# Attention to mixture in one kernel: v loaded two units ahead, a 13th early weight tile, and two small loads on another queue

## The chip, the cores and the metric

One core of a Trainium2 chip runs the whole program. The metric is the device time of one execution in microseconds (us), lower is better. All arithmetic is float32 or forms of it.

## What is computed

Three steps follow one another: a linear attention with decay over 4 batches and 8 heads, a soft mixture of 8 experts over the 3072 tokens that come out of it, and a two-layer block with `h - tanh(h)` between its layers.

```python
for b in range(nb):                                   # attention, blocks of the sequence
    intra = einsum('bhij,bhjd->bhid', (qb @ kb.T) * Dmask, vb)
    inter = einsum('bhid,bhde->bhie', qb * lam_pow, kv_state)
    out[:, :, sl] = intra + inter
    kv_state = lam_block * kv_state + einsum('bhsd,bhse->bhde', kb * rev_pow, vb)

logits = x @ phi                                      # x: attention's output, (3072, 512)
slot_input = softmax(logits, 0).T @ x                 # (32, 512)
for e in range(8):
    slot_out[e] = relu(slot_input[e] @ w1[e]) @ w2[e] # w1: 512 x 1024, w2: 1024 x 512
x = softmax(logits, 1) @ slot_out

h = x @ w_in                                          # 512 x 2048
out = (h - tanh(h)) @ w_out                           # 2048 x 512
```

## The kernel before

**Stages.** The order of all instructions is written out by hand. The attention runs 24 units u (6 blocks of 128 positions, `c = u // 4`, times 4 batches). The loop at lines 437 to 490 is skewed: iteration u holds `scores(u + 1)` (q times k), `route(u - 1)` (the output turned, and once in four units the logits) and `attend(u)` (times v, and the state). After the last unit follows a short tail that forms `si`, the slots' inputs. Then come 8 experts (`expert1`, `expert2`), PE's first matmul of them being `hp`. Then the last block, whose 96 chunks (`dps`, `s`, `r`, `ops`) need `w_in` and `w_out` decoded from 64-bit words (`wif`, `wf`, line 121) first.

**Loads.** All loads are issued by SP, in the order of the code. A unit needs `qk` (512 KB), `v` (256 KB) and, up to unit 19, k in another layout: either loaded (256 KB) or, for the units in `TURN_K`, turned on PE by `turn_k` (4 transposes) and copied by ScalarE. `load_unit(u, 0)` loads qk, `load_unit(u, 1)` k and v. Iteration u issues qk(u + 3), then `FILL[u]` half tiles of expert weights (512 KB each), then k(u + 3) and v(u + 3). qk, k and v have three buffers each, so v(u + 3) goes where v(u) lay and waits for `attend(u)`.

**The ring of weight tiles.** A weight tile is 1 MB (8 KB per partition), loaded as two halves. Tiles come from groups that become free at different times: `a` (3 tiles) and `b` (12) exist from the start, `d` (1) opens after iteration 19 in the space of the k tiles, `e` (1) after iteration 22 in that of the qk tiles, `c` (4) after the last unit in that of the rest of the attention. `RING_OF` names the group of each load in turn: 21 tiles in all before the first is used again. Tile 22 (`w1_5_1`, of expert 5) goes into an `a` tile and waits for the first matmuls `hp` of expert 0.

**In flight.** A load's issue also waits for the landing of the load eight before it, whose semaphore it takes over. So up to eight are in flight, and they land in the order of their issue.

**Start.** SP issues `lam` (4 KB), then qk and v of units 0, 1 and 2, then `phi` in four pieces of 16 KB.

Of the kernel before, what the change touches and what calls it, by code (L numbers as in the profile page):

```python
# [9 lines left out]
F32 = mybir.dt.float32  # L10
# [10 lines left out]
B, H, S, DH = 4, 8, 768, 64  # L21
P = 128
NC = S // P
NP = H // 2
DM = H * DH
# [6 lines left out]
NU = NC * B  # L32
# [30 lines left out]
LATE = 8,  # L63
LINEAR = 43, 47
CHECK = 57, 59, 63
TURN_K = [0, 1, 2, 6, 11, 16]
FILL = [2, 1, 1, 1, 1, 2, 2, 1, 1, 1, 2, 1, 1, 2, 1, 2, 1, 2, 1, 2, 3, 2, 6, 8]
RING = dict(a=3, b=12, d=1, e=1, c=4)
RING_OF = "a" * 3 + "b" * 12 + "de" + "c" * 4 + "a" * 3 + "b" * 8


@with_exitstack
def tile_main(ctx, tc, qkv, lam, phi, w1, w2, w_in, w_out, out):
    nc = tc.nc
# [135 lines left out]
    with pool("att_out") as att_out:  # L210
# [4 lines left out]
        att_qk = with_q.enter_context(pool("att_qk"))  # L215
        att_k = with_state.enter_context(pool("att_k"))
# [14 lines left out]
        qk_t, kc_t, sd_t, xt_t, xn_t = {}, {}, {}, {}, {}  # L231
        lt_ps, dn_t, al_t, dt_t = {}, {}, {}, {}

        def load_unit(u, part=None):
            if part in (None, 0):
                qk_t[u] = att_qk.tile([P, 2, NP, P], F32, tag="qk", name="qk", bufs=3)
                nc.sync.dma_start(
                    out=qk_t[u].rearrange("p t a i -> p t (a i)"), in_=qkv[u, :, 0:2])
            if part in (None, 1):
                if u // B < NC - 1 and u not in TURN_K:  # L240
                    k_t[u] = att_k.tile([P, DM], F32, tag="k", name="k", bufs=3)
                    nc.sync.dma_start(out=k_t[u], in_=qkv[u, :, 2])
                v_t[u] = v_t.get(u) or new_v()
                nc.sync.dma_start(out=v_t[u], in_=qkv[u, :, 3])

        def turn_k(u, qk, bk):
            if u in TURN_K:
# [44 lines left out]
        def attend(u):  # L292
            c, b = divmod(u, B)
            v, at = v_t.pop(u), at_t.pop(u)

            xp = [bank(3 + h2, [P, 2, P], "xp") for h2 in range(2)]
            at_head = lambda p, h2: xp[h2][p % 2 * DH:(p % 2 + 1) * DH, p // 2]
            if c > 0:
                for p in range(NP):
                    for h2 in range(2):  # L300
                        sl = slice(h2 * DH, (h2 + 1) * DH)
                        nc.tensor.matmul(  # L302
                            at_head(p, h2), st_t[b][sl, p], qs_t[u][sl, p], start=p < 2, stop=False,
                            skip_group_check=True)
            xt_t[u] = att_out.tile([P, 2, 2, P], F32, tag="xt", name="xt", bufs=5)
            for h2 in range(2):
                for p in range(NP):
                    h = 2 * p + h2
                    nc.tensor.matmul(  # L309
                        at_head(p, h2), v[:, h * DH:(h + 1) * DH], at[:, h],  # L310
                        start=c == 0 and p < 2, stop=True, skip_group_check=True)
                nc.scalar.copy(xt_t[u][:, h2], xp[h2])  # L312
            if c < NC - 1:
                up = bank(7, [P, NP, DH], "up")
                for p in range(NP):
                    for h2 in range(2):
                        h = 2 * p + h2
                        nc.tensor.matmul(  # L318
                            up[h2 * DH:(h2 + 1) * DH, p], kc_t[u][:, h],
                            v[:, h * DH:(h + 1) * DH], start=True, stop=True)  # L320
                if c == 0:
                    nc.vector.tensor_copy(st_t[b], up)
                else:
                    nc.vector.tensor_tensor(out=st_t[b], in0=up, in1=sd_t[u], op=ALU.add)  # L324
# [70 lines left out]
                    out=acc, in0=acc, scalar=al_t[c], in1=ap, op0=ALU.mult, op1=ALU.add)  # L395


        nc.sync.dma_start(out=lamb[:, :H], in_=bass.AP(tensor=lam.tensor, offset=lam.offset, ap=[[0, P], [1, H]]))
        load_unit(0, 0)
        load_unit(0, 1)  # L400
        load_unit(1, 0)
        load_unit(1, 1)
        load_unit(2, 0)
        load_unit(2, 1)
        for h2 in range(2):
            for g in range(2):
                nc.sync.dma_start(
                    out=phi_sb[g * DH:(g + 1) * DH, 2 * h2:2 * h2 + 2],
                    in_=phi[h2 * DH:(h2 + 1) * DH].rearrange("d (s g) n -> d s g n", g=2)[:, :, g])

# [25 lines left out]
                channel_multiplier=1)  # L436
        for u in range(-1, NU):
            if 3 <= u + 3 < NU:
                load_unit(u + 3, 0)
            if u >= 0:  # L440
                fill(FILL[u])
            if 3 <= u + 3 < NU:
                load_unit(u + 3, 1)
            if u + 1 < NU:
                scores(u + 1)
            if u < 0:
                turn_k(0, qk_t[0], 4)
                turn_k(1, qk_t[1], 5)
                prep_q(0)
                prep_q(1)  # L450
                prep_k(0)
            if 2 <= u + 2 < NU:
                prep_q(u + 2)
            late_route = (u - 1) // B == NC - 1
            if u >= 1 and not late_route:
                route(u - 1)
            last_of = u - 1 if u >= 1 and (u - 1) % B == B - 1 else None
            if last_of is not None:
                mm = route_max(last_of // B)
            if u >= 5 and u % B == 1:  # L460
                route_t((u - 5) // B)
            if 0 <= u < NU:
                attend(u)
                if u == 0:
                    for h2 in range(2):
                        sl = slice(h2 * DH, (h2 + 1) * DH)
                        nc.vector.tensor_copy(
                            lamb[sl, H:], lamb[sl, :H].rearrange("p (a j) -> p a j", j=2)[:, :, h2])
                    for p in range(NP):
                        powers(ql[:, p], lamb[:, H + p:H + p + 1], nil, 1.0)  # L470
                if u + 2 < NU:
                    turn_k(u + 2, qk_t[u + 2], 6 if u else 5)
                if u + 1 < NU:
                    prep_k(u + 1)
            if late_route:
                route(u - 1)
            if last_of is not None:
                route_exp(last_of // B, *mm)
            if u >= 5 and u % B == 1:
                route_acc((u - 5) // B)  # L480
            if u == NU - B - 1:
                with_state.close()
                open_ring("d", only_early, reuse_waits="tile")
            if u == NU - 2:
                with_q.close()
                open_ring("e", only_early, reuse_waits="tile")
            if u == NU - 1:
                in_attention.close()
                open_ring("c", only_early, reuse_waits="tile")
                fill()  # L490
# [37 lines left out]
        for k in range(KD):  # L528
            nc.tensor.matmul(
                sip[:, k], acc[:, k * P:(k + 1) * P], gf[:, 1], start=k == 0, stop=False,  # L530
                skip_group_check=True)
        aps = att_out.tile([P, DM], F32, tag="xt", name="aps", bufs=5)
        nc.vector.tensor_copy(aps[:, :256], ap[:, :256])
        nc.scalar.copy(aps[:, 256:], ap[:, 256:])
        for k in range(KD):
# [612 lines left out]
```

## Time and profile before

| | us |
|---|---|
| median of three runs (313.27 to 317.07) | 314.67 |
| the profiled execution, its own time | 315.38 |
| its span, first to last instruction | 313.6 |
| attention, to the last matmul with v | 109.7 |
| first matmul of the experts | 117.8 |
| first matmul of the last block | 159.1 |

The profiled execution is 1.8 us longer than its span, and 0.7 us above the median. Shares of the span: PE (TensorE) 94% busy, DVE (VectorE) 58%, ACT (ScalarE) 43%, POOL (GpSimd) 36%. TensorE's granted clock is full nearly throughout (0.996 on the mean), which is the 2.4 GHz level. A row of the timeline gives start, length, engine, line, operation, and what is written from what; in brackets stands the idle time ahead of it and who ended it.

### The profile page before, as it was taken

What the parts mean: (1) busy time and instruction counts of PE and PEld (TensorE: products, weight loads), DVE (VectorE), ACT (ScalarE), POOL (GpSimd) and SP (SyncE); (2) the same over time, 40 slices, a digit from 0 to 9 for tenths busy, and PEclk for the clock granted to TensorE, in tenths of its full rate; (3) what the DMA queues carried; (4) which work ended last, traced back from release to release, by engine and by line L of the source; (5) the groups of instructions that cost most, each with busy time, mean ns of one, the idle gap of its engine ahead of it and who ended that gap; (6) DMA issues with size and microseconds to landing.
All of it is one profiled execution on the core that took longest, in us unless ns stands there. A gap on an engine that the chain in (4) does not pass through costs nothing.

```text
span 313.6 us, 7419 instructions
## 1 busy us (share of the span) xinstructions
PE 294.5 (94%) x2999; PEld 212.6 (68%) x2999; DVE 181.2 (58%) x329; ACT 133.9 (43%) x280; POOL 112.9 (36%) x163
## 2 busy tenths in 40 slices
PE   7979999999999999999989889999999899999991
PEld 7868777877877774444356567777754677787771
DVE  4844435544553334520069759597773877968782
ACT  1434333334423332232239578576632544444420
POOL 3347647674673104110276545677500001000000
PEclk9999999999999999999999999999999999999998
DMA  6999999999999989999989847463000030303254
GB/s 202 369 399 381 370 403 368 382 382 380 387 380 386 382 267 408 397 392 401 394 319 336 299 146 287 161 244 134 2 2 0 2 134 0 134 2 134 76 192 141
DMA packets 33256, 79.77 MB, mean 254 GB/s; under 512 B 3649, under 2 KB 3905, under 8 KB 33217
## 3 DMA queue, kind: packets, MB, share of 16 engines
q1 hardware_dynamic: 33216, 79.25, 68.4%
q8 instruction: 25, 0.41, 0.5%
q14 instruction: 15, 0.11, 0.1%
HBM read 72.95 MB, written 6.29 MB: 253 GB/s over the span
## 4 chain that ended last, share of the span: by engine, by line
PE 44%; DMA 36%; DVE 9%; issue 4%; SPq 3%; POOL 1%; ACT 1%; DVEq 0%; POOLq 0%; ACTq 0%
PE ops L820 21%; DMA w<-in_w 19%; DMA qk<-in_qkv 12%; PE dps L795 5%; DVE r L813 4%; DMA wi<-in_w_in 3%; PE xp L309 3%; PE sc L285 3%; DVE part L828 2%; PE xp L302 2%; PE xnp L343 1%; PE ops L1056 1%; PE qp L872 1%; POOL top L117 1%; DMA wo<-in_w_out 1%
## 5 line engine op out<-in xcount | busy, mean ns | idle before, releaser
L820 PE MATMUL ops<-wr,r 128*128 128x512 f32 (+1 forms) x388 | 109.1, 397 | 1.2 <-ACT part L826 0.9
L820 PEld LDWEIGHTS ops<-wr,r 128*128 128x128 f32 x388 | 72.3, 188 | 22.3 <-ACT part L826 3.1
L799 ACT ACTIVATE s<-dps 128x512 f32<-128x512 f32 x96 | 56.9, 603 | 53.8 <-PE dps L795 51.3
L813 DVE SCALAR_TENSOR_TENSOR r<-dps,mt,s 128x512 fp32r<-128x512 f32 x89 | 64.9, 746 | 20.0 <-ACT s L799 19.2
L795 PE MATMUL dps<-c,ms 128*128 128x512 f32 x96 | 39.5, 425 | 3.8 <-DVE r L813 1.9
L289 DVE TENSOR_TENSOR at<-sc,dtab 128x512 f32<-128x512 f32 x48 | 30.9, 684 | 15.6 <-PE sc L285 15.6
L257 POOL TENSOR_TENSOR qs<-qk,ql 128x512 f32<-128x512 f32 x20 | 25.8, 1291 | 34.9 <-DMA qk<-in_qkv 31.7
L345 ACT COPY xn<-xnp 128x512 f32<-128x512 f32 x24 | 14.1, 586 | 43.6 <-PE xnp L343 43.6
L285 PE MATMUL sc<-qk 64*128 64x128 f32 x384 | 27.9, 285 | 4.2 <-DMA qk<-in_qkv 4.2
L285 PEld LDWEIGHTS sc<-qk 64*128 64x128 f32 x384 | 23.3, 187 | 10.7 <-DMA qk<-in_qkv 6.0
L795 PEld LDWEIGHTS dps<-c,ms 128*128 128x128 f32 x96 | 17.9, 188 | 15.2 <-DVE r L813 7.4
L309 PE MATMUL xp<-at,v 128*64 128x128 f32 x384 | 26.3, 279 | 0.0
L264 POOL TENSOR_TENSOR kc<-k,dtab 128x512 f32<-128x512 f32 x20 | 21.2, 1061 | 11.3 <-ACT k L252 5.2
L312 ACT COPY xt<-xp 128x256 f32<-128x256 f32 x48 | 17.8, 373 | 16.5 <-PE xp L309 16.0
L309 PEld LDWEIGHTS xp<-at,v 128*64 128x64 f32 x384 | 20.5, 136 | 4.1 <-issue 3.8
L324 DVE TENSOR_TENSOR st<-up,sd 128x256 f32<-128x256 f32 x16 | 6.8, 425 | 25.6 <-PE up L318 25.6
L828 DVE TENSOR_TENSOR part<-ops,part 128x512 f32<-128x512 f32 (+1 forms) x29 | 17.9, 666 | 0.9 <-PE ops L1056 0.9
L576 PE MATMUL hp<-w,si 128*32 128x256 f32 x256 | 16.1, 383 | 1.3 <-DMA w<-in_w 1.3
L117 POOL CAST top<-wi 128x512 f16<-128x512 bf16 x16 | 14.6, 922 | 6.0 <-DMA wi<-in_w_in 4.7
L600 PE MATMUL op<-w,hz 128*32 128x512 f32 x128 | 16.5, 594 | 0.0
L121 DVE SCALAR_TENSOR_TENSOR wif<-wi,top 128x512 uint32<-128x512 uint32 x16 | 13.2, 834 | 5.4 <-POOL top L117 5.4
L117 POOL CAST top<-wo 128x512 f16<-128x512 bf16 x16 | 15.1, 967 | 3.1 <-DMA wo<-in_w_out 3.1
(181 smaller groups left out, 339.9 us busy)
## 6 DMA issues: line engine op xcount, KB each, us to landing
w<-in_w SPq DMA_DIRECT2D x64, 512.0 KB, 9.2
qk<-in_qkv SPq DMA_DIRECT2D x24, 512.0 KB, 7.6
wi<-in_w_in SPq DMA_DIRECT2D x16, 512.0 KB, 4.7
wo<-in_w_out SPq DMA_DIRECT2D x16, 512.0 KB, 4.3
v<-in_qkv SPq DMA_DIRECT2D x24, 256.0 KB, 7.1
out<-part SPq DMA_DIRECT2D x23, 256.0 KB, 2.2
k<-in_qkv SPq DMA_DIRECT2D x14, 256.0 KB, 8.4
out<-part SPq DMA_DIRECT2D x2, 128.0 KB, 3.5
```

The costliest lines, as they stand in the source:

```text
L117: nc.gpsimd.tensor_copy(out=every(top().bitcast(F16), 2, 1)[:, sl], in_=every(raw().bitcast(BF16)[:, 4:], 4, 0)[:, sl])
L257: nc.gpsimd.tensor_tensor(out=qs_t[u], in0=qk_t[u][:, 0], in1=ql, op=ALU.mult)
L264: nc.gpsimd.tensor_tensor(out=kc_t[u], in0=k_t.pop(u).rearrange("p (h d) -> p h d", h=H), in1=kd, op=ALU.mult)
L285: nc.tensor.matmul(sc[h2][:, p], qk[sl, 1, p], qk[sl, 0, p], start=True, stop=True)
L289: nc.vector.tensor_tensor(out=by_head(at_t[u], h2), in0=sc[h2], in1=by_head(dtab, h2), op=ALU.mult)
L309: nc.tensor.matmul(at_head(p, h2), v[:, h * DH:(h + 1) * DH], at[:, h], start=c == 0 and p < 2, stop=True, skip_group_check=True)
L312: nc.scalar.copy(xt_t[u][:, h2], xp[h2])
L795: nc.tensor.matmul(d_t[n], ms[:, f * P:(f + 1) * P], c4[:, c], start=True, stop=True)
L799: nc.scalar.activation(out=s, in_=d_t[n], func=AF.Square, scale=math.sqrt(1.0 / 3))
L813: nc.vector.scalar_tensor_tensor(out=r_t[n], in0=d, scalar=mt[:, f, NS:], in1=s, op0=ALU.add, op1=ALU.mult)
L820: nc.tensor.matmul(op, r_t[n][:, t * P:(t + 1) * P], wr_t[f // 2][:, f % 2, sl], start=first, stop=last)
L828: nc.vector.tensor_tensor(out=pt, in0=op, in1=pt, op=ALU.add)
```

## The change

Four edits, made together.

1. `lam` and the four pieces of `phi` are issued by ScalarE's queue, ahead of anything else there.
2. `load_unit` becomes `load_qk` (qk and k) and `load_v`. Iteration u issues qk(u + 3) and k(u + 3), then the weights, then v(u + 2). Only v(0) and v(1) are loaded ahead of the loop.
3. `b` has 13 tiles and `c` 3; `RING_OF` follows, still with 21 tiles. `FILL` issues its 12th half tile one iteration later and the following ones earlier: by iteration 20 it has issued 32 halves, where it had 31. The output tiles `xt` have 4 buffers for 5, which gives 2 KB per partition back.
4. k is turned for units 0, 1, 2, 6, 10, 14 and 18 (7), not 0, 1, 2, 6, 11 and 16 (6): 13 loads of k for 14.

```diff
-TURN_K = [0, 1, 2, 6, 11, 16]
-FILL = [2, 1, 1, 1, 1, 2, 2, 1, 1, 1, 2, 1, 1, 2, 1, 2, 1, 2, 1, 2, 3, 2, 6, 8]
-RING = dict(a=3, b=12, d=1, e=1, c=4)
-RING_OF = "a" * 3 + "b" * 12 + "de" + "c" * 4 + "a" * 3 + "b" * 8
+TURN_K = [0, 1, 2, 6, 10, 14, 18]
+FILL = [2, 1, 1, 1, 1, 2, 1, 2, 1, 2, 1, 2, 1, 2, 1, 2, 1, 2, 1, 2, 3, 2, 6, 8]
+RING = dict(a=3, b=13, d=1, e=1, c=3)
+RING_OF = "a" * 3 + "b" * 13 + "de" + "c" * 3 + "a" * 3 + "b" * 8
...
-        nc.sync.dma_start(out=lamb[:, :H], ...)
-        load_unit(0, 0)
-        load_unit(0, 1)
-        load_unit(1, 0)
-        load_unit(1, 1)
-        load_unit(2, 0)
-        load_unit(2, 1)
+        nc.scalar.dma_start(out=lamb[:, :H], ...)
+        load_qk(0)
+        load_v(0)
+        load_qk(1)
+        load_v(1)
+        load_qk(2)
...
-                nc.sync.dma_start(out=phi_sb[...], ...)
+                nc.scalar.dma_start(out=phi_sb[...], ...)
...
             if 3 <= u + 3 < NU:
-                load_unit(u + 3, 0)
+                load_qk(u + 3)
             if u >= 0:
                 fill(FILL[u])
-            if 3 <= u + 3 < NU:
-                load_unit(u + 3, 1)
+            if 2 <= u + 2 < NU and u >= 0:
+                load_v(u + 2)
```

On SP, at the start of the program, the order changes as follows (a row is an instruction with its line, what it writes and from where; `-` before, `+` after; the numbers behind the names tell buffers apart).

```order
-L398 DMA lamb_96<-in_lam 128x8
-L237 DMA qk_98<-in_qkv 128x1024
+L236 DMA qk_98<-in_qkv 128x1024
 L244 DMA v_92<-in_qkv 128x512
-L237 DMA qk_101<-in_qkv 128x1024
+L236 DMA qk_101<-in_qkv 128x1024
 L244 DMA v_103<-in_qkv 128x512
-L237 DMA qk_105<-in_qkv 128x1024
-L244 DMA v_107<-in_qkv 128x512
-L407 DMA phi_sb_95<-in_phi 64x2x32 x4
-L237 DMA qk_183<-in_qkv 128x1024
+L236 DMA qk_105<-in_qkv 128x1024
+L236 DMA qk_181<-in_qkv 128x1024
```

The first load of SP is now qk(0), and qk(3) (`qk_183`, now `qk_181`) stands right behind qk(2), with v(2) and `phi` gone from between them. v(1) there and the three loads behind it now take over the semaphores of `lam` and of `phi`, and wait for their landing.

On SP, at the end of the attention, before: from qk(22) (`qk_1545`) on, with v(22) (`v_1550`), qk(23) (`qk_1609`) and v(23) (`v_1616`), the last load that the attention needs. `w1_4_0` is the tile of group `e`, `w1_4_1` the first of group `c`.

```order
L237 DMA qk_1545<-in_qkv 128x1024
L156 DMA w1_3_1_1547<-in_w1 128x1024 x2
L244 DMA v_1550<-in_qkv 128x512
L237 DMA qk_1609<-in_qkv 128x1024
L165 DMA w2_3_0_1611<-in_w2 128x2x512 x2
L165 DMA w2_3_1_1614<-in_w2 128x2x512
L244 DMA v_1616<-in_qkv 128x512
L165 DMA w2_3_1_1614<-in_w2 128x2x512
L156 DMA w1_4_0_1789<-in_w1 128x1024 x2
L156 DMA w1_4_1_1824<-in_w1 128x1024 x2
```

The same place of the changed kernel, from v(21) (`v_1555`) on: qk(23) is `qk_1614`, v(22) `v_1620`, v(23) `v_1697`. `w1_4_0` is now the tile of group `d`, `w1_4_1` that of `e`, `w2_4_0` the first of `c`.

```order
L244 DMA v_1555<-in_qkv 128x512
L236 DMA qk_1614<-in_qkv 128x1024
L165 DMA w2_3_0_1553<-in_w2 128x2x512
L165 DMA w2_3_1_1617<-in_w2 128x2x512 x2
L244 DMA v_1620<-in_qkv 128x512
L156 DMA w1_4_0_1694<-in_w1 128x1024 x2
L244 DMA v_1697<-in_qkv 128x512
L156 DMA w1_4_1_1797<-in_w1 128x1024 x2
L165 DMA w2_4_0_1832<-in_w2 128x2x512 x2
```

v(22) has moved from ahead of qk(23) to behind it and behind three halves of weights; ahead of v(23) stand 34 halves of weights, not 31, and behind it, ahead of group `c`, two halves and not three.

## Rows read from the trace of the kernel before

**Rows 1.** Chain that ended last, in time: start, length, what.

```profile
114.01 12.22 DMA w<-in_w
...
147.24 10.65 DMA wi<-in_w_in
```

**Rows 2.** Stretches: us, busy us (count) by engine, clock, DMA share, GB/s.

```profile
24.00:104.00 80.00, 78.07 (x1395) 62.86 (x1395) 37.91 (x74) 29.45 (x81) 48.09 (x51) 1.00 1.03 382
108.00:116.00 8.00, 7.79 (x104) 5.77 (x103) 2.48 (x11) 4.00 (x12) 0.00 (x0) 1.00 0.81 261
126.00:157.00 31.00, 29.69 (x330) 12.43 (x322) 6.04 (x18) 7.78 (x15) 4.25 (x10) 1.00 1.04 396
```

**Rows 3.** Timeline of SP's issues: start, length, line, what, count.

```profile
0.75 0.39 SPq L398 DMA_DIRECT2D lamb<-in_lam  x1
1.20 0.42 SPq L237 DMA_DIRECT2D qk<-in_qkv  x1
...
4.37 2.88 SPq L407 DMA_DIRECT2D phi_sb<-in_phi  x4
...
100.13 0.34 SPq L244 DMA_DIRECT2D v<-in_qkv  x1
```

**Rows 4.** Single DMA issues (from 1.20, 95.15, 100.13, 102.51, 109.80, 111.11): KB, us to landing.

```profile
qk<-in_qkv SPq DMA_DIRECT2D x1, 512.0 KB, 4.8
...
v<-in_qkv SPq DMA_DIRECT2D x1, 256.0 KB, 7.3
...
v<-in_qkv SPq DMA_DIRECT2D x1, 256.0 KB, 8.3
...
w<-in_w SPq DMA_DIRECT2D x1, 512.0 KB, 9.8
...
w<-in_w SPq DMA_DIRECT2D x1, 512.0 KB, 3.7
...
w<-in_w SPq DMA_DIRECT2D x1, 512.0 KB, 7.0
```

**Rows 5.** Waits of SP: who, for whom, us in total, times, longest.

```profile
SPq L244 <- PE up L318: 25.6, 16, 2.5
```

**Rows 6.** Timeline of PE, end of the attention and first expert.

```profile
106.42 1.09 PE L309 MATMUL xp<-at,v 128*64 128x128 f32 x16
107.44 0.66 PE L343 MATMUL xnp<-cst,xt 128*128 128x128 f32 x4
108.03 0.67 PE L302 MATMUL xp<-qs,st 64*64 64x128 f32 x16
108.62 1.09 PE L309 MATMUL xp<-at,v 128*64 128x128 f32 x16
109.65 0.66 PE L343 MATMUL xnp<-cst,xt 128*128 128x128 f32 x4
...
117.81 1.93 PE L576 MATMUL hp<-w,si 128*32 128x256 f32 x32
```

**Rows 7.** Timeline of PE, experts 6 and 7, and start of the last block.

```profile
142.22 1.93 PE L576 MATMUL hp<-w,si 128*32 128x256 f32 x32
143.97 1.90 PE L600 MATMUL op<-w,hz 128*32 128x512 f32 x16
...
146.60 1.30 PE L576 MATMUL hp<-w,si 128*32 128x256 f32 x16
...
149.83 0.64 PE L576 MATMUL hp<-w,si 128*32 128x256 f32 x8 [0.65 <-DMA w<-in_w]
150.29 1.90 PE L600 MATMUL op<-w,hz 128*32 128x512 f32 x16
...
159.11 1.10 PE L743 MATMUL mp__2401<-wif,so 128*32 128x128 f32 x16
```

**Rows 8.** Timeline of DVE, the last decode ahead of the last block.

```profile
158.83 0.69 DVE L121 SCALAR_TENSOR_TENSOR wif<-wi,top 128x512 uint32<-128x512 uint32 x1 [0.65 <-POOL top L117]
```

**Rows 9.** The page's costliest groups: busy us, mean ns of one, idle before.

```profile
L285 PE MATMUL sc<-qk 64*128 64x128 f32 x384 | 27.9, 285 | 4.2 <-DMA qk<-in_qkv 4.2
```

**Rows 10.** ACT's timeline at the start, and one turned k of PE's.

```profile
0.75 1.28 ACT L252 ACT_TABLE_LOAD   x1 [0.75 <-PEq L1138]
7.86 0.59 ACT L252 COPY k<-kp 128x512 f32<-128x512 f32 x1 [5.83 <-PE kp L250]
...
11.21 0.66 PE L250 MATMUL kp<-cst,qk 128*128 128x128 f32 x4
```

**Rows 11.** Uses of v: min/median/max ns, first and last start in us.

```profile
L309 PE MATMUL xp<-at,v x384: 272/273/323, 9.7 to 109.4; 128*64 128x128 f32 x192
```

More of the change, by code (lines that the diff above doesn't have):

```diff
@@ L232, in tile_main, with load_qk, load_v @@
         lt_ps, dn_t, al_t, dt_t = {}, {}, {}, {}
[L234 to L244, printed above, removed]
+        def load_qk(u):
+            qk_t[u] = att_qk.tile([P, 2, NP, P], F32, tag="qk", name="qk", bufs=3)
+            nc.sync.dma_start(
+                out=qk_t[u].rearrange("p t a i -> p t (a i)"), in_=qkv[u, :, 0:2])
+            if u // B < NC - 1 and u not in TURN_K:
+                k_t[u] = att_k.tile([P, DM], F32, tag="k", name="k", bufs=3)
+                nc.sync.dma_start(out=k_t[u], in_=qkv[u, :, 2])
+        def load_v(u):
+            v_t[u] = v_t.get(u) or new_v()
+            nc.sync.dma_start(out=v_t[u], in_=qkv[u, :, 3])
         def turn_k(u, qk, bk):
@@ L304, in attend @@
                             skip_group_check=True)
-            xt_t[u] = att_out.tile([P, 2, 2, P], F32, tag="xt", name="xt", bufs=5)
+            xt_t[u] = att_out.tile([P, 2, 2, P], F32, tag="xt", name="xt", bufs=4)
             for h2 in range(2):
@@ L395, in route_acc @@
                     out=acc, in0=acc, scalar=al_t[c], in1=ap, op0=ALU.mult, op1=ALU.add)
-        nc.sync.dma_start(out=lamb[:, :H], in_=bass.AP(tensor=lam.tensor, offset=lam.offset, ap=[[0, P], [1, H]]))
-        load_unit(0, 0)
-        load_unit(0, 1)
-        load_unit(1, 0)
-        load_unit(1, 1)
-        load_unit(2, 0)
-        load_unit(2, 1)
+        nc.scalar.dma_start(
+            out=lamb[:, :H], in_=bass.AP(tensor=lam.tensor, offset=lam.offset, ap=[[0, P], [1, H]]))
+        load_qk(0)
[3 more added lines that the diff above has]
+        load_qk(2)
         for h2 in range(2):
             for g in range(2):
-                nc.sync.dma_start(
+                nc.scalar.dma_start(
                     out=phi_sb[g * DH:(g + 1) * DH, 2 * h2:2 * h2 + 2],
@@ L531, in tile_main @@
                 skip_group_check=True)
-        aps = att_out.tile([P, DM], F32, tag="xt", name="aps", bufs=5)
+        aps = att_out.tile([P, DM], F32, tag="xt", name="aps", bufs=4)
         nc.vector.tensor_copy(aps[:, :256], ap[:, :256])
```

## The prediction

> **What bounds the kernel now.** I read the chain of waits first, then the stretches, then the single loads with their landing, then PE's timeline at the two ends of the experts. The chain leads through the experts by loads, `w` after `w` and then `wi` [rows 1], so up to about 158 us the end hangs on the stream of loads. The stretches say how full that stream is: 382 GB/s over the attention and 396 over the experts, with a DMA share of 1.03 and 1.04, and between them a dip to 261 GB/s [rows 2]. A rate of 382 GB/s is 0.686 us for 256 KB; I call that a unit of the stream. A load in the full stream needs 7 to 10 us to land, one that meets an empty queue 3.7 us [rows 4]: the queue in front of the engines is deep, and what a load finds ahead of it sets its landing.
>
> PE is nearly full beside it. It is busy 78.1 of 80 us in the attention [rows 2], and its score matmuls wait 4.2 us in all for qk [rows 9]. In the experts it runs from 117.81 us [rows 6] without a wait for weights until expert 7. There `hp` takes from 146.60 to 150.29 = 3.69 us where expert 6 took 142.22 to 143.97 = 1.75 us [rows 7]: 1.94 us of waiting, for the last tiles of the stream. So two clocks run to the last block: PE's, from the last v to `hp` and through eight experts, and the stream's. Today the stream is late by 1.94 us, and no more; that is all PE can gain in the experts, and also what it can lose for nothing.
>
> **The change, part by part.**
>
> *lam and phi by ScalarE.* SP's first load starts at 0.75, not 1.20 us [rows 3]: the stream starts 0.45 us earlier. The 2.88 us that SP spends on `phi` [rows 3] are no gain of the stream: six loads lie ahead of them, the first lands at 1.20 + 4.8 = 6.0 us [rows 4], and the other five keep the engines going beyond 10 us. On ScalarE the five issues cost 0.39 + 2.88 = 3.3 us ahead of the table load of 1.28 us, to about 5.3 us; its first work is at 7.86 after 5.83 us of idleness [rows 10], so nothing. Were that cover gone, the first copy would be late by up to 3.3 us. What is new is that v(1) waits for `lam` and qk(2), qk(3) and k(3) each for a piece of `phi`; the loads ahead, landing to about 8 us, cover a wait of two to three us.
> The Trainium skill (DMA: Bandwidth & Descriptors, Issuing engines are not separate DMA queues) says that issuing from several engines saves only the issuing time, since all use the same 16 DMA engines. By that rule `phi`'s bytes still cost the stream their time, which is how I count; if all 3.3 us were saved for the stream instead, v(23) below would land 2.9 us earlier and the gain rival would hold. No row here has two queues at work.
>
> *One more k turned.* One unit less in the stream, 0.7 us. PE gets four transposes, 0.66 us [rows 10], ScalarE a copy of 0.59 us. PE pays that in the attention unless it is waiting anyway; below it is.
>
> *v one unit later, and behind the weights.* SP's waits for `attend` ahead of v (25.6 us, 16 times [rows 5]) go, but they cost nothing: the queue stays full behind them at 382 GB/s. What moves is the place of v in the stream. Ahead of v(23) stand three halves of weights more (six units) and one k less: five units, 5 x 0.686 = 3.4 us. It landed at 100.13 + 8.3 = 108.4 [rows 3, 4], and PE took it at 108.62 [rows 6], 0.2 us later: no slack. Now it lands at 108.4 + 3.4 - 0.45 = 111.4. v(22) has nine units more ahead of it (qk(23), four halves, less one k): 95.15 + 7.3 = 102.5 [rows 4] becomes 102.5 + 6.2 - 0.45 = 108.2, where PE wants it at 106.42 [rows 6]. PE then does 1.09 + 0.59 + 0.59 us and stands at about 110.5 before v(23), so v(23) decides: the last use of v starts at 111.4, not 108.62, **2.8 us later**. From there to `hp` nothing changes (108.62 to 117.81): `hp` starts at 120.6.
> Bounds: at 396 GB/s the five units are 3.3 us; with twice as much lost or gained at the start, 0 to 0.9 us, the shift is 2.3 to 3.2 us. The low end without any wait for v is the rival below.
> The Trainium skill (Perfetto Trace Analysis, Roofline) puts a core's ceiling at about 435 GB/s, the sum of its 16 DMA engines. Here 382 and 396 were measured; at 435 the five units would be 3.0 us and the sum 0.4 us less.
>
> *The 13th tile.* Half a tile more has been issued by iteration 20, and the loads that can be issued before the attention ends grow from 34 to 36 halves. But with v(23) late, only two halves lie behind it: the queue holds work until about 111.4 + 4 x 0.66 = 114.1 us, and group `c` opens at 111.4 + 1.1 = 112.5 us, its first load landing 3.7 us later [rows 4], at 116.2. Before, the last load ahead of `c` landed at 102.51 + 9.8 = 112.3, and the first of `c` at 109.80 + 3.7 = 113.5 [rows 4]. So the dip is moved, not filled. `w2_4_0` begins to land at 116.2, not 111.11 + 7.0 = 118.1 [rows 4]; if the slow restart repeats (the two loads behind the first of `c` took 118.1 - 113.5 = 4.6 us, where four units at 396 GB/s are 2.6), the one behind it is back where it was. The stream of the experts is therefore 0 to 2 us earlier, not later. The tile behind `c` waits for `hp`, as before, with the 3.7 us to land well inside the six loads of `c` (8 us).
>
> *Sum.* `hp` + 2.8; expert 7's wait is gone, since the stream isn't later and PE comes later: - 1.94; so the end of the experts + 0.9 us. The last block begins with `mp` at 159.11, whose second half needs the decode ending at 159.52 [rows 7, 8]; 0.9 us later for PE, not later for the decode: + 0.9. From there all is in order and moves along. 315.38 + 0.9 = 316.3 for an execution like the profiled one, which lies 0.7 above the median: **315.6 us**. With the bounds (shift 2.3 to 3.2; wait absorbed 1.0 to 1.94 if a part of it stays) + 0.4 to + 2.2: 315.1 to 316.9. The spread of the three runs (313.27 to 317.07) widens this to 314.0 to 317.5.
>
> **Rivals.**
>
> *The dip is filled and v is in time (gain).* For it: the dip cost (382 - 261) x 8 us = 0.97 MB, 2.5 us; one k and the start give 1.1; v has slack in most units, since v(22) landed 3.9 us ahead of its use (102.5 against 106.42). It holds if v(23) lands before about 109. If PE reaches `hp` as before, it saves the 1.94 us of expert 7: 312.7. If PE also loses its waits for qk (4.2, less 0.66), the stream's 3.6 us are the limit: 311.1. Against it: three halves more ahead of v(23), in a stream that lands in order.
>
> *SP is held by k (slower).* k(u + 3) now stands ahead of the weights and of v(u + 2). For k(5), 9, 13 and 17 the buffer is that of k(u + 1), which POOL reads only at the end of iteration u: SP stands still for most of a unit, (109.4 - 9.7) / 23 = 4.3 us [rows 11], and v(u + 2) is issued with two units, 8.7 us, to its use, where a landing takes 7.3 to 8.3 us [rows 4]. Up to 1 us each for units 4, 8, 12, 16 or the ones they push, 4 us in all if the stream falls back with them: 315.6 + 2 to 4 = 317.6 to 319.6. It decides once a stand is longer than the loads in flight last, about 8 us. Against it: before, SP stood up to 2.5 us [rows 5], and the rate stayed.
>
> *Nothing moves:* late v and fewer bytes cancel: 314.7, inside my range.
>
> **Chances.** Forecast (314.0 to 317.5) 0.68; gain (311.0 to 314.0) 0.17; held by k (317.5 to 320) 0.12; else 0.03. Eight in ten: 313.0 to 317.7. About 1% (3.1 us) is what a measurement of this kernel can tell from no change. Below 311.5: the lower end of the gain, 0.07. Above 317.8: most of the second rival, 0.10. Within: 0.83.
>
> **What would show it.** Right: PE waits for v ahead of the last two uses of v; the last one starts near 111.4 and `hp` near 120.6; no wait for weights in expert 7; the dip lies at about 112 to 118 us; SP has no waits for `attend`. Wrong: v(23) lands before 109.5, or `hp` starts before 118; then the gain rival. If SP waits on POOL for whole units and the rate over the attention falls below 370 GB/s, it is the second.

## The result, and the profile after

| | before | changed |
|---|---|---|
| median, us (20 runs each) | 315.45 (313.27 to 317.21) | 318.09 (316.48 to 318.99) |
| ratio, 95% interval | 1 | 1.0077 (1.0056 to 1.0098) |
| profiled execution, us | 315.38 | 316.81; in a second profile 318.42 |

The change costs 0.8%, 2.6 us between the medians. The forecast was + 0.9 us, 315.6, with a range up to 317.7: the sign was right, the size was not, and the median lies 0.4 us above the range. The first profiled execution of the changed kernel is 1.3 us below its median, the second, taken later beside other kernels, 0.3 above it; both are read here. In two experiments TensorE's granted clock goes to its lower level, 1.2 GHz, for 3.4 us behind a wait of PE: in `e3_tile_only`, whose profile is not read, from 80.34 us on, and at the start of `e1_queue_back`, from 19.39.

PE's timeline after, first execution: the last two uses of v, `hp`, expert 7, start of the last block.

```profile
108.49 1.09 PE L309 MATMUL xp<-at,v 128*64 128x128 f32 x16 [0.86 <-DMA v<-in_qkv]
111.77 1.09 PE L309 MATMUL xp<-at,v 128*64 128x128 f32 x16 [1.00 <-DMA v<-in_qkv]
120.95 1.93 PE L576 MATMUL hp<-w,si 128*32 128x256 f32 x32
...
149.74 1.93 PE L576 MATMUL hp<-w,si 128*32 128x256 f32 x32
151.49 1.90 PE L600 MATMUL op<-w,hz 128*32 128x512 f32 x16
...
160.31 1.07 PE L743 MATMUL mp__2406<-wif,so 128*32 128x128 f32 x16
```

These answer to [rows 6, 7]. The path is the forecast one. PE waits for v at its last two uses; the last starts at 111.77 where 111.4 was forecast (before: 108.62), `hp` at 120.95 (forecast 120.6), and expert 7 takes 151.49 - 149.74 = 1.75 us, without a wait for weights. The second execution has the same rows, a microsecond later.

```profile
109.56 1.09 PE L309 MATMUL xp<-at,v 128*64 128x128 f32 x16 [1.63 <-DMA v<-in_qkv]
112.85 1.09 PE L309 MATMUL xp<-at,v 128*64 128x128 f32 x16 [1.01 <-DMA v<-in_qkv]
122.02 1.93 PE L576 MATMUL hp<-w,si 128*32 128x256 f32 x32
...
161.38 0.85 PE L743 MATMUL mp__2406<-wif,so 128*32 128x128 f32 x12
```

The stretches after, first execution (us, busy us and count of PE, PEld, DVE, ACT, POOL, clock, DMA share, GB/s), answering to [rows 2], and the first 16 us of before, not shown so far.

```profile
0.00:16.00 16.00, 13.32 (x132) 11.88 (x134) 9.18 (x22) 4.35 (x7) 4.56 (x14) 1.00 0.76 241
24.00:104.00 80.00, 79.14 (x1421) 64.28 (x1419) 37.33 (x75) 29.75 (x81) 49.12 (x51) 1.00 1.04 391
...
108.00:116.00 8.00, 6.33 (x97) 4.91 (x97) 1.11 (x6) 3.14 (x9) 0.00 (x0) 1.00 0.75 275
126.00:157.00 31.00, 31.00 (x358) 13.94 (x351) 8.59 (x25) 9.16 (x18) 3.88 (x9) 1.00 1.03 393
```

```profile
0.00:16.00 16.00, 14.03 (x168) 12.53 (x168) 9.64 (x23) 5.12 (x9) 5.34 (x15) 1.00 0.87 289
```

Two things are here that the forecast doesn't have. The first 16 us move (289 - 241) x 16 = 0.77 MB less than before, 2 us of the stream; and the attention runs at 391 GB/s, not 382, which gives (391 - 382) x 80 = 0.72 MB back. The two nearly cancel in the landing of v(23), so that the forecast of the first execution (316.3, measured 316.81) came out well by luck.

SP's timeline at the start after. In [rows 3] `lam` went first; the line of v(1) there, and the landing of `lam`:

```profile
2.61 0.43 SPq L244 DMA_DIRECT2D v<-in_qkv  x1
...
lamb<-in_lam SPq DMA_DIRECT2D x1, 4.0 KB, 2.7
```

After:

```profile
0.75 0.39 SPq L236 DMA_DIRECT2D qk<-in_qkv  x1
1.20 0.41 SPq L244 DMA_DIRECT2D v<-in_qkv  x1
1.66 0.43 SPq L236 DMA_DIRECT2D qk<-in_qkv  x1
6.29 0.33 SPq L244 DMA_DIRECT2D v<-in_qkv  x1
```

And two single loads of after, both issued at 0.75 us: KB, us to landing.

```profile
qk<-in_qkv SPq DMA_DIRECT2D x1, 512.0 KB, 5.3
lamb<-in_lam ACTq DMA_DIRECT2D x1, 4.0 KB, 5.5
```

v(1) is issued at 6.29, after a wait of 4.2 us for `lam`. SP's waits after, up to 110 us (who, for whom, us in total, times, longest), which answer to [rows 5]:

```profile
SPq L240 <- POOL kc L264: 11.5, 7, 3.0
...
SPq L244 <- DMA lamb<-in_lam: 4.2, 1, 4.2
```

And two groups of PE's (busy us, mean ns, idle time before), which answer to [rows 9]:

```profile
L285 PE MATMUL sc<-qk 64*128 64x128 f32 x384 | 27.9, 285 | 0.0
L309 PE MATMUL xp<-at,v 128*64 128x128 f32 x384 | 26.3, 279 | 3.7 <-DMA v<-in_qkv 3.7
```

SP no longer waits 25.6 us for `attend` [rows 5]; it waits 11.5 us for POOL ahead of k, 3.0 us at most. PE's scores no longer wait 4.2 us for qk; PE waits 3.7 us for v, 1.9 of them at the last two uses (and, at the start, 1.6 us for qk ahead of two turned k).

### The profile page after: what moved, and what is told of

It is laid out like the page before. It is cut to its first block, busy times and chain, and to the rows that moved or that the text cites. A ratio compares the mean times of both kernels' runs of the same rounds, so it can differ in the third digit from the quotient of the medians.

```text
span 315.0 us, 7426 instructions
## 1 busy us (share of the span) xinstructions
PE 295.7 (94%) x3003; PEld 214.7 (68%) x3003; DVE 180.3 (57%) x329; ACT 134.4 (43%) x281; POOL 112.3 (36%) x163
## 3 DMA queue, kind: packets, MB, share of 16 engines
HBM read 72.68 MB, written 6.29 MB: 251 GB/s over the span
## 4 chain that ended last, share of the span: by engine, by line
PE 76%; DMA 10%; DVE 8%; ACT 2%; issue 2%; DVEq 0%; ACTq 0%; SPq 0%
PE ops L820 24%; DMA v<-in_qkv 8%; PE dps L795 7%; PE sc L285 6%; PE xp L309 6%; PE op L600 5%; PE hp L576 5%; PE xnp L343 3%; DVE r L813 3%; PE xp L302 3%; PE up L318 2%; DVE part L828 2%; DMA qk<-in_qkv 2%; PE ltp L332 2%; PE wp L423 2%
## 5 line engine op out<-in xcount | busy, mean ns | idle before, releaser
L343 PE MATMUL xnp<-cst,xt 128*128 128x128 f32 x96 | 15.7, 286 | 0.0
```

Of the source, the lines that this page charges most:

```text
L343: nc.tensor.transpose(xnp[:, p], xt[:, p // 2, p % 2], ident)
```

## The experiments

Sixteen kernels, the changed one again among them, four at a time on one chip, each timed against before there (35 or 34 executions of before, 11 or 12 of each kernel). The groups ran on four chips, so kernels of two groups are compared by their ratios to before. In the expectations, theories A, S and Q let the start count beside the place of the last v; for B and P only that place counts, and the start is made good.

### The four edits apart

`e1_queue_back`: the changed kernel with `lam` and `phi` on SP again.

```diff
-        nc.scalar.dma_start(out=lamb...)   # and phi
+        nc.sync.dma_start(out=lamb...)     # and phi
```

> The changed kernel with lam and phi back on SP's queue, where they stood (edit 1 undone, all else as changed). In the trace of the changed kernel v(1) waited 4.2 us for lam's landing, and the stream ran thin until about 14 us. Theory A (the start and v's place both count): the stream is some 2 us ahead again, v(23) lands near 110, hp starts near 119, and the time is 1.5 to 2 us below the changed kernel's: about 316.3 (ratio to before 1.002 to 1.004). Theory B (only v's place counts, the start is made good before the end of the attention): within 0.5 us of the changed kernel, ratio 1.006 to 1.009, hp near 121.

Measured: 1.0065 (1.0039 to 1.0092). 266 GB/s in the first 16 us, v(23) used from 111.39. That is B's number: putting the loads back wins 0.4 us against 1.0077, 1.0 us against the 1.0098 of `e8_changed` below, neither clear of the noise, as long as v(23) is late.

`e2_queue_only`: before with that edit alone, in the other direction.

> The kernel before with lam and phi on ScalarE's queue and nothing else. Theory A: v(1), qk(2), v(2) wait for the landing of lam and phi, the stream loses about 2 us by 15 us, v(23), which had 0.2 us of slack, lands 1.5 to 2 us later, hp too; the experts' loads are late by the same, so the 1.9 us of waiting in expert 7 stay: ratio 1.004 to 1.007 (+1.3 to +2.2 us). Theory B: no difference beyond 0.5 us, ratio 0.998 to 1.002.

Measured: 1.0081 (1.0042 to 1.012), as much as the whole change, though v is three units ahead; that is above theory A's 1.004 to 1.007, which the interval still holds, and B's made-good start is refuted for this order. v(1) is issued at 6.31, 246 GB/s in the first 16 us, and the last v starts at 110.08, 1.5 us later than before. Its profiled execution (315.23) lies 1.8 below its median.

`e3_tile_only`: before with the 13th tile, the table and `TURN_K` of the change (edits 3 and 4).

> The kernel before with edits 3 and 4 alone: 13 tiles in b, 3 in c, the new FILL, xt with 4 buffers, k turned for 7 units; v stays three ahead behind k, lam and phi stay on SP. Theory A: v(23) has one unit more ahead of it than before (two for a half tile, less one k), 0.7 us; behind it lie four halves, so the queue holds work until group c opens and the dip shrinks by 1 to 2 us; hp +0.6, expert 7 waits less by up to 1.9: ratio 0.994 to 0.998 (-0.6 to -1.9 us). Rival C (the 13th tile itself costs: the stream is no earlier, or the tile behind c waits for hp longer): ratio 1.001 to 1.005.

Measured: 1.0016 (0.9982 to 1.0051). Theory A's range (up to 0.998) is just left out, rival C's is held; without a profile to read, what these edits do by themselves stays open.

`e4_v_only`: before with edit 2 alone.

> The kernel before with edit 2 alone: qk and k of three units ahead, then weights, then v of two units ahead; 12 tiles in b, old FILL and TURN_K, lam and phi on SP. Theory A: v(22) has eight units more ahead of it, lands near 108, the last use of v starts near 110.3 and hp near 119.5 (+1.7), group c opens 1.7 us later and the dip is longer by as much, so the stream is late too and expert 7 goes on waiting: ratio 1.003 to 1.006 (+1 to +1.9 us). Theory B agrees. Rival C expects this one to be no slower than before, 0.998 to 1.001.

Measured: 1.0054 (1.0022 to 1.0085), the last v from 110.06, forecast 110.3; rival C's 0.998 to 1.001 is excluded. The three parts make 0.81 + 0.16 + 0.54 = 1.5% (to some 0.6%), the whole 0.8%. That a stream late for two reasons is late only once, at the last v, would explain it; it is argued, not shown.

### The place of v(23), and the start

`e5_v2_first`: `e1_queue_back` with v(2) ahead of the loop.

```diff
         load_qk(2)
+        load_v(2)
...
-            if 2 <= u + 2 < NU and u >= 0:
+            if 3 <= u + 2 < NU and u >= 0:
                 load_v(u + 2)
```

> The changed kernel with lam and phi back on SP (as in the run that put them back, 1.0065 of before) and with v(2) loaded ahead of the loop again, right behind qk(2); from v(3) on v stays two units ahead and behind the weights. Theory S (the start costs: v(2) stands behind qk(3), k(3) and two halves of weights, SP waits for the first scores ahead of them, and the stream runs thin): 0 to 16 us goes from 266 back to about 289 GB/s, the second wait of PE at 18.5 us is gone, the stream is 0.5 MB ahead, v(23) lands about 1 us earlier, near 110, and the time is 1.002 to 1.004 of before. Theory P (only the place of the last v behind the weights counts, PE makes the start good by waiting less later): PE's wait at the start is gone too, but v(23) lands at 111 as before and the time stays at 1.005 to 1.008.

Measured: 1.005 (1.002 to 1.0079). 277 GB/s at the start; PE takes v(2) at 16.80, v(23) at 111.00. The interval holds both theories; the late v(23) is P's.

`e6_v_ahead`: as that, with each v ahead of its iteration's weights (`load_v(u + 2)` moved above `fill(FILL[u])`).

> As the run beside it (lam and phi on SP, v(2) ahead of the loop), and each v(u + 2) is issued ahead of the weights of iteration u, not behind them. Ahead of v(23) stand 32 halves of weights, not 34 (before: 31), and one k less than before: half a MB of weights more, 256 KB of k less, so 0.7 us more of the stream than before. SP waits for the attend of the unit ahead again, for v(u - 1)'s buffer. Theory P: v(23) lands at 108.4 + 0.7 = 109 or, with the 392 GB/s of the runs with v two units ahead, at 107 to 108, PE reaches the experts as before or up to 1 us later, the dip at 108 to 116 us is filled in part, and the time is 0.996 to 1.001 of before. Theory S: the start is as before too, so it says the same. Rival C (the 13th tile costs by itself): 1.002 to 1.005 in spite of v in time.

Measured: 1.0021 (0.999 to 1.0052); the last v from 108.95 after 0.42 us of waiting. The mechanism is P's, the median is above P's 0.996 to 1.001, which the interval still holds; rival C's number would fit too, but `e16_12_tiles`, below, has the 13th tile as a gain once v is in time.

`e7_fill_late`: the changed kernel with a table that puts 30 halves ahead of v(23), not 34.

```diff
-FILL = [..., 2, 1, 2, 3, 2, 6, 8]
+FILL = [..., 2, 1, 2, 1, 0, 10, 8]
```

> The changed kernel with lam and phi on ScalarE's queue and v(2) behind the weights as it is; only the table is changed, so that iterations 20, 21, 22 issue 1, 0 and 10 halves of weights, not 3, 2 and 6. Ahead of v(23) stand 30 halves, not 34, and behind it four, to the end of the attention. Theory P: v(23) lands four halves earlier, 4 x 1.34 = 5.4 us less than 111.6, so by 107 it is no longer waited for; PE starts the experts near 118, and the time is 0.996 to 1.001 of before. Theory S: v(23) is in time too, but the stream's loss at the start stays, PE has lost some 1.5 to 2 us at the start that nothing gives back, hp starts at 119 to 120, and the time is 1.003 to 1.006.

`e8_changed`: the changed kernel again, on the same chip.

> The changed kernel itself, nothing altered, beside the others on the same chip, for a second profile. All theories: 1.0056 to 1.0098 of before, as it was measured. If the median's 1.3 us above the first profiled execution come from a later v(23) and hp (spread of the stream), this execution shows v(23) landing beyond 111.6 and hp beyond 121; if they come from the part behind the experts, hp starts at 121 again and the first matmul of the last block beyond 161.

Measured: 1.0011 (0.9982 to 1.0039) for `e7_fill_late` and 1.0098 (1.0062 to 1.0134) for `e8_changed`. Three numbers in a table are worth 0.87%, 2.7 us. PE with the late table, at the end of the attention and the start of the last block:

```profile
108.70 1.09 PE L309 MATMUL xp<-at,v 128*64 128x128 f32 x16
117.88 1.93 PE L576 MATMUL hp<-w,si 128*32 128x256 f32 x32
...
157.25 1.07 PE L743 MATMUL mp__2406<-wif,so 128*32 128x128 f32 x16
```

The stretch from 104 to 118 us, with the late table and then of `e8_changed`:

```profile
104.00:118.00 14.00, 13.79 (x180) 10.20 (x176) 5.11 (x18) 5.24 (x15) 0.70 (x1) 1.00 1.01 385
```

```profile
104.00:118.00 14.00, 11.16 (x162) 8.11 (x156) 3.60 (x11) 5.33 (x14) 1.29 (x1) 1.00 0.75 272
```

With the late table v(23) lands at 106.47, 2.2 us ahead of its use; there is no wait for v at the last uses, none in the experts, and the dip is filled: 385 GB/s against 272. `hp` at 117.88 is P's; S had 119 to 120. This is the gain rival's mechanism, reached by the table, but not its time: that was 312.7, 0.994 of before, and 1.0011 is no gain. `e8_changed` also answers its own question: of the 1.61 us between the two profiles of the changed kernel 1.07 come from a later v(23) (landed at 112.71, not 111.63) and `hp` (122.02), so from the spread of the stream; 0.54 lie behind the experts.

### With v(23) in time

`e9_late_sp`: `e7_fill_late` with `lam` and `phi` on SP.

> The changed kernel with the late table (iterations 20 to 22 issue 1, 0 and 10 halves of weights), as the run that measured 1.0011 of before, and lam and phi back on SP. So v(23) is in time and edit 1 is undone. Theory P (PE's waits at the start are given back over the attention, since it waits less later; only the end of the attention counts): the last v at 108.7 and hp at 117.9 as with lam and phi on ScalarE, 1.000 to 1.003. Theory Q (with v in time the start shows: SP stands 4.2 us for lam there, the stream of 0 to 16 us is 243 GB/s): 266 GB/s from 0 to 16 us, the last v 0.3 to 1 us earlier, 0.996 to 1.000.

`e10_late_v2`: that, with v(2) ahead of the loop as in `e5_v2_first`.

> As the run beside it (late table, lam and phi on SP), and v(2) loaded ahead of the loop, right behind qk(2). Theory P: 1.000 to 1.003 again, the same as the two others with the late table. Theory Q: 277 GB/s from 0 to 16 us as in the run with v(2) first, PE takes v(2) at 16.7 us and not at 18.6, the last v starts at 107 to 108, hp at 116 to 117, no wait for weights in the experts (in the late-table run there was none), 0.993 to 0.998.

`e11_late_v_ahead`: that, with v ahead of its iteration's weights as in `e6_v_ahead`.

> Late table, lam and phi on SP, v(2) ahead of the loop, and each v(u + 2) ahead of its iteration's weights: the start of before (289 GB/s from 0 to 16 us), v two units ahead but never behind the weights of its iteration, 30 halves ahead of v(23) (before 31). Theory P: 1.000 to 1.003. Theory Q: the least of the four, PE takes v(3) at 20.2 us or earlier, last v at 107 to 108, hp at 116 to 117, 0.992 to 0.997.

`e12_late_three`: before with edits 3 and 4 and the late table; v three units ahead.

> The kernel before with the 13th tile, the seventh turned k and the late table, and nothing else: lam and phi on SP, v three units ahead as before, 30 halves ahead of v(23). It says whether v two units ahead is needed for the gain. If the place of the last v and the filled dip are all (P): v(23) lands by 108.4, PE waits for qk as before (4 us in all), hp at 117.8, no wait for weights in expert 7, 0.993 to 0.998 of before. If v two ahead brings something of its own (the 392 GB/s over the attention where three ahead had 382 to 384, PE's waits for qk gone): 0.998 to 1.002, later than the runs beside it by 0.3% or more.

Measured, on one chip: 0.996 (0.9927 to 0.9992), **0.9916 (0.9885 to 0.9946)**, 0.9954 (0.992 to 0.9987) and 0.9998 (0.997 to 1.0026). `e10_late_v2` beats both kernels: 312.96 us, 2.6 less than before there. It differs from `e12_late_three` only in edit 2, without its start: v two units ahead, and k ahead of the weights. First PE's score group, SP's longest wait, the attention's rate and PE's last v of `e12_late_three`:

```profile
L285 PE MATMUL sc<-qk 64*128 64x128 f32 x384 | 27.9, 285 | 5.1 <-DMA qk<-in_qkv 5.1
```

```profile
SPq L244 <- PE up L318: 28.8, 17, 3.4
```

```profile
24.00:104.00 80.00, 77.36 (x1389) 62.65 (x1387) 35.94 (x74) 29.23 (x79) 48.39 (x50) 1.00 1.01 374
```

```profile
110.08 1.09 PE L309 MATMUL xp<-at,v 128*64 128x128 f32 x16
```

Then PE's two groups, the rate and PE's timeline in `e10_late_v2`:

```profile
L285 PE MATMUL sc<-qk 64*128 64x128 f32 x384 | 28.2, 287 | 0.8 <-DMA qk<-in_qkv 0.8
L309 PE MATMUL xp<-at,v 128*64 128x128 f32 x384 | 26.3, 279 | 1.0 <-DMA v<-in_qkv 1.0
```

```profile
24.00:104.00 80.00, 79.92 (x1413) 64.06 (x1411) 35.92 (x76) 30.56 (x82) 49.79 (x51) 1.00 1.03 390
```

```profile
107.71 1.09 PE L309 MATMUL xp<-at,v 128*64 128x128 f32 x16
116.88 1.93 PE L576 MATMUL hp<-w,si 128*32 128x256 f32 x32
...
156.24 1.07 PE L743 MATMUL mp__2406<-wif,so 128*32 128x128 f32 x16
```

With v three ahead, PE waits 5.1 us for qk, behind SP's 28.8 us of waiting for `attend`, though v(23) lands at 107.49 and is not waited for; with v two ahead PE waits 0.8 + 1.0 us, the rate is 390 GB/s for 374, and the last v starts 2.4 us earlier. So edit 2 brings something of its own. P's mechanism for `e12_late_three` (`hp` at 117.8) is refuted, since `hp` starts at 119.25; its time (0.993 to 0.998) is touched only by the interval's end. Whether the place of v or that of k carries the gain was not tried apart. Theory Q holds for `e9_late_sp` (0.996), and `e10_late_v2` is a little better than it said. The time of `e11_late_v_ahead` is in Q's range, but it is not the least of the four as Q had it, and its last v (108.39) and `hp` (117.56) are later than Q's: there SP waits for `attend` again (5.6 us), and PE waits 2.2 us for qk.

### lam, phi, and the 13th tile

Four kernels from `e10_late_v2`, with what was then open. `e13_lam_act`: `lam` alone by ScalarE.

> The fastest kernel so far (late table, v(2) ahead of the loop, lam and phi on SP, 0.9916 of before) with lam alone on ScalarE's queue. Theory L (lam's landing is what costs: on SP it landed at 3.3 us, on ScalarE's queue at 6.3, behind qk(0), and v(1) stands on SP until then): v(1) is issued at 6.3 and not at 2.6 us, 0 to 16 us falls from 273 to 240 to 250 GB/s, and the time is 0.994 to 0.999. Theory F (phi's landing costs): as without the edit, 0.989 to 0.994. Theory N (neither costs once v is in time): 0.989 to 0.994 with the same stall.

`e14_phi_act`: `phi` alone.

> The same kernel with phi alone on ScalarE's queue; lam is SP's first load. Theory L: phi's pieces land in time behind the loads ahead of them, SP is free 2.9 us earlier for qk(3) unless the first scores hold it, and the time is 0.988 to 0.994. Theory F: a load of SP stands for phi's landing at 7 to 9 us, 0 to 16 us falls to 240 to 260 GB/s, 0.994 to 0.999. Theory N: 0.989 to 0.994.

`e15_both_act`: both, which is edit 1.

> The same kernel with lam and phi both on ScalarE's queue, which is edit 1 by itself with v in time. Theory L: as lam alone, 0.994 to 0.999. Theory F: as phi alone, 0.994 to 0.999. Theory N: 0.989 to 0.994.

Measured: 0.9963 (0.9926 to 1.0), 0.9949 (0.9914 to 0.9984) and 1.0001 (0.9974 to 1.0029), where `e10_late_v2` had 0.9916. Theory N is refuted for both together: edit 1 costs 0.85% (to some 0.4%). By the medians `lam` has 0.5 and `phi` 0.3% of it, neither certain by itself (the intervals overlap that of `e10_late_v2`). The profiles, one execution of each, show a later end of the attention only where `phi` moved: PE's last v in `e13_lam_act`, `e14_phi_act` and `e15_both_act`, where `e10_late_v2` had 107.71:

```profile
107.40 1.09 PE L309 MATMUL xp<-at,v 128*64 128x128 f32 x16
...
108.84 1.09 PE L309 MATMUL xp<-at,v 128*64 128x128 f32 x16
...
109.72 1.09 PE L309 MATMUL xp<-at,v 128*64 128x128 f32 x16
```

SP's timeline at the start with `phi` on ScalarE, then with both, and the first 16 us of the latter:

```profile
2.16 0.62 SPq L236 DMA_DIRECT2D qk<-in_qkv  x1
3.54 0.33 SPq L244 DMA_DIRECT2D v<-in_qkv  x1
3.91 0.51 SPq L236 DMA_DIRECT2D qk<-in_qkv  x1
5.87 0.33 SPq L244 DMA_DIRECT2D v<-in_qkv  x1
```

```profile
1.66 0.43 SPq L236 DMA_DIRECT2D qk<-in_qkv  x1
6.50 0.33 SPq L244 DMA_DIRECT2D v<-in_qkv  x1
6.87 0.43 SPq L236 DMA_DIRECT2D qk<-in_qkv  x1
```

```profile
0.00:16.00 16.00, 12.93 (x136) 11.53 (x138) 9.22 (x22) 4.50 (x8) 4.56 (x14) 1.00 0.75 243
```

With `phi` there, v(1) waits until 3.54 for the first piece of `phi` and v(2) until 5.87 for the second; with both, v(1) stands until 6.50. L was wrong in the place for `lam` alone: v(1) is issued at 2.13, and it is a piece of `phi` on SP that waits 2.0 us for `lam`; the first 16 us are at 273 GB/s, not below 250. `lam` lands as late there (5.8 us after its issue) as with both, so it is not its landing alone that thins the stream: a load of v has to wait for it.

`e16_12_tiles`: `e10_late_v2` with 12 tiles, `c` of 4 and the six turned k of before, and a table with 30 halves ahead of v(23).

```diff
+TURN_K = [0, 1, 2, 6, 11, 16]
+FILL = [..., 2, 1, 2, 2, 0, 9, 8]
+RING = dict(a=3, b=12, d=1, e=1, c=4)
```

> The same kernel (lam and phi on SP, v(2) ahead of the loop) with 12 tiles in b, 4 in c, xt of 5 buffers and six turned k, as before; the table issues 30 halves ahead of v(23) as there and four behind it, so that 34 and not 36 halves can be issued before group c opens. If the 13th tile is part of the gain: the stream runs out before the first load of c lands, 104 to 118 us falls from 380 to some 350 GB/s, expert 7 waits for weights by 0.5 to 1.5 us, 0.994 to 0.998. If the place of v alone made it: 0.990 to 0.994, no wait in the experts. The k that is loaded again costs the stream 0.7 us, and PE is spared 0.66 us: about nothing either way.

Measured: 0.9962 (0.9934 to 0.999), 0.46% behind `e10_late_v2`. Its stretch from 104 to 118 us, and expert 7:

```profile
104.00:118.00 14.00, 13.52 (x188) 10.32 (x188) 5.23 (x19) 4.74 (x14) 0.65 (x3) 1.00 0.92 343
```

```profile
147.75 0.64 PE L576 MATMUL hp<-w,si 128*32 128x256 f32 x8 [0.37 <-DMA w<-in_w]
```

The dip (343 GB/s against 380 in `e10_late_v2`) and the wait in expert 7 are back: the 13th tile, with the seventh turned k and its table, is a gain once v is in time, just clear of the noise (0.46%, to some 0.4%; from `hp` to `mp` the profiles give 39.95 - 39.36 = 0.6 us of it). Which of the edits carries it was not tried.

### The steps in a row

Each kernel differs from the one above it in what the column of steps says. The last column is the row at which PE takes the last v.

| kernel | ratio | step | last v, us |
|---|---|---|---|
| before | 1 | | 108.62 |
| `e12_late_three` | 0.9998 | 13 tiles, 7 turned k, late table | 110.08 |
| `e10_late_v2` | 0.9916 | edit 2: v two ahead from v(3) on, k ahead of the weights | 107.71 |
| `e9_late_sp` | 0.996 | v(2) too, behind weights | 107.64 |
| `e7_fill_late` | 1.0011 | `lam`, `phi` by ScalarE | 108.70 |
| `e8_changed` | 1.0098 | the table of the change | 112.85 |

In microseconds (1% is 3.15): - 0.1, - 2.6, + 1.4, + 1.6, + 2.7. With half intervals of about 0.3% on each ratio a step is known to some 0.45%, 1.4 us, and only the second and the last are well clear of that; the place of v(2) stays open, since the two profiled executions (312.96 both) show nothing of it.

## Why the prediction missed

*Right: the place of v(23).* The loads that now lie ahead of it make it late, PE takes it as it lands, and from there to `hp` nothing changes: 120.95 - 111.77 = 9.18 us, as 117.81 - 108.62 = 9.19 before. `e7_fill_late` shows it from the other side: with four halves less ahead of it v(23) lands at 106.47, and `hp` starts at 117.88.

*Right: the wait of expert 7 goes.* From `hp` to `mp` it is 160.31 - 120.95 = 39.36 us, before 159.11 - 117.81 = 41.30: 1.94 us, as forecast. The dip was moved, not filled, and behind it the first load of `c` landed at 117.09 (forecast 116.2).

*Mis-sized: the shift, `hp` + 2.8.* Forecast + 2.8 (bounds 2.3 to 3.2), measured + 3.15 and + 4.23 in the two executions. With - 1.94 and what lies behind `mp` (156.27 us before, 156.50 and 157.04 after) that makes + 1.4 and + 3.0; the median is + 2.6. "From there all is in order and moves along" put nothing on the last block. It takes 156.3 to 157.2 us over all the profiles, in no order of 12 or 13 tiles (`e4_v_only` 156.53, `e13_lam_act` 156.41, `e5_v2_first` 157.21): a spread that the sum did not have, its cause open.

*Mis-sized: the base.* The three runs had a median of 314.67, the twenty have 315.45, so the profiled execution lay at the median and not 0.7 above it. Of the 2.5 us between 315.6 and 318.09 this is 0.8; the sum itself missed by 1.7.

*Failed: "the loads ahead, landing to about 8 us, cover a wait of two to three us".* This step put the start at - 0.45 us. The wait is 4.2 us, since `lam` landed 5.5 us after its issue and not 2.7 as on SP, and the first 16 us moved 0.77 MB less, part of it by v(2) behind the weights (266 GB/s with `lam` and `phi` back on SP, in `e1_queue_back`). And covering must be reckoned to the landing, not to the issue: qk(1), the last load ahead, landed at 8.61, v(1), issued at 6.29, at 10.50. With v in time the step costs 0.85%; with v(23) late it is hardly to be seen (`e1_queue_back`). That the stream starts 0.45 us earlier failed too: qk(0), issued at 0.75, took 5.3 us and landed at 6.09, before from 1.20 at 6.04 [rows 4].
The Trainium skill (DMA: Bandwidth & Descriptors, Issuing engines are not separate DMA queues) says that transfers of several engines interleave on the same 16 DMA engines. The trace agrees: the 128 packets of `lam` (32 bytes each) start from 2.5 to 5.9 us, among those of qk(0), with which it was issued (1.8 to 5.3 us), and `lam` lands 0.2 us behind it; ahead of qk(0) on SP's queue they started from 1.8 to 3.0 us. The prediction drew from this rule only that nothing is won, not that a small load gets slower by it.

*Failed: SP's waits for `attend` "cost nothing: the queue stays full".* A rate of 382 GB/s was read as full, and it wasn't: 391 without those waits, and the step from `e12_late_three` (374) to `e10_late_v2` (390) gives 2.6 us. Making good a thin start is not the reason: `e2_queue_only` starts as thin, has v three ahead and stays at 384. The argument looked at whether the queue empties; what counts, as I read it, is when qk, queued behind a v that waits, gets issued. PE's 4.2 us for qk [rows 9] were the trace of it: they are 0.0 to 0.8 in the kernels with v behind the weights, and 3.1 and 2.2 in `e6_v_ahead` and `e11_late_v_ahead`, where v waits for `attend` again.

*Missed: PE without slack hands the spread on.* From v(21) on PE takes every v within 0.8 us of its landing. In the second execution the six loads from the landing of qk(21) to that of v(21) took 7.5 us where they took 6.5 in the first, and all that follows is 1.1 us later. The forecast took one execution's rate as the rate.

Of the rivals, the gain needs the late table and `lam` and `phi` on SP (0.996 in `e9_late_sp`). The other, SP held by k, has its wait (11.5 us, 3.0 at most) but not its price: the rate did not fall, and between v(3) and v(22) PE waits for v once, 0.43 us.

## What to carry to other kernels

A load's place in one long queue is a price in microseconds of what now lies ahead of it; when it is moved behind bulk loads, look at its last use, where nothing comes later to make it good, and let the bulk loads give way there. Where several edits touch one stream, look whether a gain in one (here edit 2) is eaten by another (the table, the start); undo them in a row, since measured one by one from before they don't add up. And see which loads wait for the landing of a small one: issued on a second queue together with a big load, it shares the engines with that and lands when that lands.

## What the runs showed of the hardware

A load of 4 KB lands 2.6 to 2.7 us after its issue when it goes first on SP's queue, and 5.5 to 5.8 us when ScalarE's queue issues it in the same moment as SP issues 512 KB; it then lands 0.2 us behind that load. The 512 KB, in turn, took 5.3 to 5.6 us beside it and 4.5 to 5.0 us behind it. So the second queue made both slower here. It is not slow by itself: in `e14_phi_act`, where ScalarE issued the first piece of `phi` (16 KB) in the same moment as SP issued the 4 KB of `lam`, it took

```profile
phi_sb<-in_phi ACTq DMA_DIRECT2D x1, 16.0 KB, 2.8
```

A wait of PE can cost more than its length. In `e3_tile_only` PE waited 1.97 us for qk, to 80.10 us, and TensorE's granted clock was at 0.5, 1.2 GHz, from 80.34 to 83.75; in `e1_queue_back` it waited 1.88 us for v, to 18.58, and the clock was at 0.5 from 19.39 to 22.81. No other profile has the lower level between 6 and 300 us; the longest wait for a load there is 1.80 us, for qk in `e12_late_three`. Whether this is part of the spread between executions no run here shows.
